# Scores of two query steps at once, and the last queries beside the last keys: a threshold-attention kernel with an ELU feed-forward network on one core

## The chip, the cores and the metric

The kernel runs on one core of one Trainium2 chip. The metric is the device time of one execution in microseconds, taken as the median of several runs. A profiled execution gives, beside it, the span from the first to the last instruction and what each engine did.

## The reference

```python
# q, k, v: (8, 8, 576, 64) fp32; tau: a scalar; w_in (512, 2048), w_out (2048, 512)
scores = scale * np.matmul(q, k.transpose(0, 1, 3, 2))          # scale = 1/8
thresh = np.max(scores, axis=-1, keepdims=True) - tau
scores = np.where(scores >= thresh, scores, -1000000000.0)
attn = np.exp(scores - np.max(scores, axis=-1, keepdims=True))
attn = attn / (np.sum(attn, axis=-1, keepdims=True) + 1e-09)
attn_out = np.matmul(attn, v)
x = attn_out.transpose(0, 2, 1, 3).reshape(4608, 512)           # heads side by side
h = x @ w_in
g = np.where(h > 0.0, h, np.exp(np.minimum(h, 0.0)) - 1.0)      # ELU
out = g @ w_out
```

## The kernel before

**Units of work.** Two heads of one batch entry form a pair; there are 32 pairs, four to a batch entry. A pair has 576 queries: four steps (i = 0 to 3) of 128 queries with both heads, and a fifth (i = 4) that holds the last 64 queries of both heads in one tile of 128 rows (`qd`, a tile with the two 64-row blocks on its diagonal). The last 64 keys of a head are its "last keys".

**One step.** `scores` (L236) writes 2 x 288 columns per head to PSUM; the two heads use the upper and the lower 64 rows of TensorE. Then for each head: VectorE takes the maximum (`max_of`, L276), GpSimd computes the threshold (`bound_of`, L280), ScalarE the bias `nb` (L285) and the exponential into a tile `e` (L287), VectorE masks it into `w` and sums it in one instruction (`mask_of`, L296), then takes the reciprocal (L302, L303), and GpSimd normalizes (L272). A step later `turn_squares` transposes `w` on VectorE in 32 x 32 squares into a tile `x` (L380, L390) and sends it to DRAM in four DMAs (L393); two steps later `fetch` (L401, L403) reads it back as `wTa` (steps 0 and 1) or `wTb` (steps 2 to 4), now with keys on the partitions. `values` multiplies with v in two parts: one matmul for the last keys (L416, `vd` holds the last 64 rows of both heads' v on its diagonal) and eight with 64 output rows (L420). `values_out` copies the result to `xt`.

**FFN.** It works on 512 tokens of a batch entry at a time, with products of half-size blocks (seven products in place of eight). `first_product` (L955) has seven quarters for each of eight blocks, `second_round` (L1110) twice 28; a quarter is two or four matmul records, about 0.86 us of TensorE. A batch entry makes 112 quarters, 28 for each pair. After the products ScalarE and VectorE move them out of three PSUM banks, and exp, minus one and the ELU follow on ScalarE, GpSimd and VectorE (L988, L993, L1002, L1010). Sums of blocks run on GpSimd (L1047) from a queue `extra`; `sums_x` (L846 to L848) on VectorE, once per batch entry.

**Order.** There are stages: the first four pairs alone, some pairs with a plain FFN and the weights' preparation, and from the tenth pair on (step `MIDDLE`) attention of pairs 9 to 31 beside the FFN of batch entries 1 to 6; then FFN alone. In the stage from `MIDDLE` on the order on each engine comes from an agenda: `on_pe(cost, f)` puts work on TensorE and moves a clock by an assumed cost, `at(t, f)` puts the other work in the order of its planned time. The engines then run their lists in order and wait by semaphores. TensorE's order for a pair was

```python
QUARTERS = ((4, 4), (4, 2), (4, 0), (4, 2), (4, 0))   # FFN quarters before and behind the values, per step
on_pe(1.25, lambda: scores(pr, i, hs))                # each step
end = on_pe(3.1 if part else 2.3, lambda: loc.update(out=values(pr, part)))   # behind steps 4 and 2
```

PSUM in this stage holds three banks for the FFN, four for scores (two tiles of two banks) and one for values.

## Time and profile before

| | |
|---|---|
| median of 3 runs | 1367.07 us (1367.02 to 1367.55) |
| profiled execution, first to last instruction | 1366.1 us |
| granted TensorE clock, mean | 0.994 |
| TensorE matmul busy | 1340.4 us (98%) |
| VectorE busy | 1064.7 us (78%) |
| ScalarE busy | 638.5 us (47%) |
| GpSimd busy | 825.2 us (60%) |
| DMA | 259.84 MB, mean 190 GB/s |

A line of a group reads: source line, engine (PE TensorE, PEld its weight loads, DVE VectorE, ACT ScalarE, POOL GpSimd, SP the DMA queue's engine), operation, output and inputs by the program's names, shapes, count, then busy time in us and the mean of one in ns, then idle time before it and what ended that idle time. In the line of a tile `f` is the FFN's PSUM, `sc` the scores', `pv` the values', `rt` that of transposes.

### The profile page before, as it was taken

Reading aid. Unit: us, or ns where it says so; the run is one execution under the profiler, and the core shown is the slowest. Engines: PE = TensorE matmul, PEld = TensorE weight load, DVE = VectorE, ACT = ScalarE, POOL = GpSimd, SP = SyncE. Lnnn points to the kernel's source line nnn. Section 1 sums busy time; section 2 is a strip of 40 time slices with the busy share of each in tenths; the row PEclk is TensorE's granted clock in tenths of the full one; section 3 lists DMA queues with packets and bytes.
Section 4 is the critical chain, followed back from the end, with each engine's and each line's share of the span. In section 5 each row is a group of like instructions: output and inputs, shape, how many; then the busy total and the mean of one; then the engine's idle time right before and its main releaser. Section 6 shows DMA issues by size and latency. Waiting matters only on the chain.

```text
span 1366.1 us, 22394 instructions
## 1 busy us (share of the span) xinstructions
PE 1340.4 (98%) x6796; PEld 1008.9 (74%) x6796; DVE 1064.7 (78%) x2344; ACT 638.5 (47%) x1418; POOL 825.2 (60%) x1322
## 2 busy tenths in 40 slices
PE   8998999999999999999999999999999999999998
PEld 7665746747777777777777777777777777888886
DVE  6879895988888887888798978888898875445433
ACT  5777675226354445545453636363636452412320
POOL 4657673878657574757475747675675646525423
PEclk9999999999999999999999999999999999999999
DMA  5254451688888989798889888897889785412211
GB/s 116 59 108 137 132 151 43 198 247 256 237 251 239 260 229 259 206 267 247 230 234 263 236 238 241 245 269 203 245 225 266 218 258 155 135 59 66 93 59 31
DMA packets 316343, 259.84 MB, mean 190 GB/s; under 512 B 208320, under 2 KB 272320, under 8 KB 316224
## 3 DMA queue, kind: packets, MB, share of 16 engines
q1 hardware_dynamic: 313856, 258.13, 67.6%
q8 instruction: 54, 0.88, 0.3%
q10 hardware_dynamic: 2368, 0.30, 0.2%
q14 instruction: 65, 0.53, 0.1%
HBM read 167.84 MB, written 90.51 MB: 189 GB/s over the span
## 4 chain that ended last, share of the span: by engine, by line
PE 89%; DVE 4%; ACT 2%; POOL 2%; issue 1%; DMA 0%; ACTq 0%; DVEq 0%; POOLq 0%; SPq 0%
PE f L1110 28%; PE f L955 28%; PE sc L236 13%; PE pv L420 9%; PE f L507 3%; PE rt L306 3%; PE pv L416 3%; PE f L467 2%; DVE mx L276 1%; POOL w L272 1%; DVE w L296 1%; ACT e L287 1%; DVE wtop L142 0%; ACT wTa L322 0%; DVE wtop L137 0%
## 5 line engine op out<-in xcount | busy, mean ns | idle before, releaser
L272 POOL TENSOR_SCALAR w<-w,rs 128x576 f32<-128x576 f32 x288 | 248.4, 867 | 120.7 <-DVE rs L303 99.9
L276 DVE TENSOR_REDUCE mx<-sc 128x1 f32<-128x576 f32 x270 | 192.8, 750 | 89.0 <-PE sc L236 88.8
L296 DVE SCALAR_TENSOR_TENSOR w<-sc,th,e 128x576 f32<-128x576 f32 x270 | 212.8, 811 | 26.7 <-ACT e L287 10.0
L287 ACT ACTIVATE e<-sc,nb,keep 128x576 f32<-128x576 f32 x270 | 223.0, 831 | 9.2 <-POOL nb L612 0.7
L285 ACT ACTIVATE nb<-mx,nkeep 128x1 f32<-128x1 f32 x254 | 75.2, 296 | 256.4 <-DVE mx L276 256.4
L380 DVE STREAM_TRANSPOSE x<-w 128x512 f32<-128x512 f32 (+1 forms) x350 | 182.6, 568 | 8.2 <-POOL w L272 8.2
L236 PE MATMUL sc<-kT,qT 64*128 64x288 f32 x1024 | 166.7, 431 | 9.0 <-DVE w L296 6.1
L236 PEld LDWEIGHTS sc<-kT,qT 64*128 64x128 f32 x1024 | 92.8, 187 | 71.4 <-issue 49.4
L280 POOL TENSOR_SCALAR th<-mx,ntau 128x1 f32<-128x1 f32 x270 | 75.7, 281 | 114.0 <-DVE mx L276 113.3
L955 PE MATMUL f<-xt,sw 128*128 128x256 f32 x512 | 128.9, 389 | 0.5 <-DVE g L977 0.5
L955 PE MATMUL f<-xt,w_in_sb 128*128 128x256 f32 x512 | 124.5, 382 | 0.3 <-ACT w L969 0.2
L955 PEld LDWEIGHTS f<-xt,sw 128*128 128x128 f32 x512 | 93.3, 190 | 28.9 <-issue 13.5
L955 PEld LDWEIGHTS f<-xt,w_in_sb 128*128 128x128 f32 x512 | 96.1, 190 | 18.9 <-ACT xs L432 4.6
L1110 PE MATMUL f<-w_out_sb,s 128*128 128x256 f32 x448 | 109.4, 387 | 0.0
L1110 PE MATMUL f<-w_out_sb,g 128*128 128x256 f32 x448 | 107.6, 382 | 0.5 <-DVE g L1010 0.5
L1110 PE MATMUL f<-t,s 128*128 128x256 f32 x448 | 106.6, 380 | 0.3 <-POOL s L1047 0.3
L955 PE MATMUL f<-x,w_in_sb 128*128 128x256 f32 x448 | 105.8, 379 | 0.0
L1110 PEld LDWEIGHTS f<-w_out_sb,s 128*128 128x128 f32 x448 | 82.3, 190 | 23.0 <-issue 11.3
L1110 PEld LDWEIGHTS f<-w_out_sb,g 128*128 128x128 f32 x448 | 83.8, 190 | 16.9 <-issue 4.2
L974 POOL TENSOR_TENSOR u<-u,w 128x256 f32<-128x256 f32 x64 | 48.9, 764 | 76.5 <-ACT u L969 76.5
L1110 PEld LDWEIGHTS f<-t,s 128*128 128x128 f32 x448 | 84.1, 190 | 13.7 <-POOL s L1047 2.7
L955 PEld LDWEIGHTS f<-x,w_in_sb 128*128 128x128 f32 x448 | 85.1, 190 | 11.6
(165 smaller groups left out, 2435.4 us busy)
## 6 DMA issues: line engine op xcount, KB each, us to landing
there<-x SPq DMA_DIRECT2D x500, 144.0 KB, 4.2
wTb<-there SPq DMA_DIRECT2D x75, 576.0 KB, 4.9
wTa<-there SPq DMA_DIRECT2D x50, 576.0 KB, 4.3
sw<-win_sums SPq DMA_DIRECT2D x62, 384.0 KB, 4.6
t<-wout_sums SPq DMA_DIRECT2D x45, 512.0 KB, 5.6
qm<-in_q_dram SPq DMA_DIRECT2D x128, 72.0 KB, 4.2
vm<-in_v_dram SPq DMA_DIRECT2D x64, 128.0 KB, 4.3
wst<-in_moe_w_in_dram SPq DMA_DIRECT2D x16, 512.0 KB, 4.3
```

The lines of the kernel that those rows point to most:

```text
L236: nc.tensor.matmul(scs[h][:, a, :HALF], qs[r], kT[r, k0 : k0 + HALF], start=True, stop=True)
L272: nc.gpsimd.tensor_scalar(wv, wv, st["rs"][:, h : h + 1], 1.0, ALU.mult, ALU.mult)
L276: nc.vector.tensor_reduce(st["mx"][:, h : h + 1], st[h][:, :, :HALF], axis=AX.XY, op=ALU.max)
L280: nc.gpsimd.tensor_scalar(st["th"][:, h : h + 1], st["mx"][:, h : h + 1], 1.0, ntau, ALU.mult, ALU.add)
L285: nc.scalar.mul(st["nb"][:, h : h + 1], st["mx"][:, h : h + 1], nkeep)
L287: nc.scalar.activation(e, st[h][:, :, :HALF], AF.Exp, bias=st["nb"][:, h : h + 1], scale=keep)
L296: nc.vector.scalar_tensor_tensor(wv, sc[:, :, :HALF], st["th"][:, h : h + 1], e, ALU.is_ge, ALU.mult, accum_out=st["sm"][:, h : h + 1])
L380: nc.vector.transpose(x[:, :, c0 : c0 + nc_], src.rearrange("p (c g n) -> p g c n", c=nc_, n=T))
L420: nc.tensor.matmul(pv[h * D : (h + 1) * D, g0 * T : g1 * T], vm[:, h, c], wT[:, g0:g1, h * (NC + 1) + c], start=False, stop=(c == NC - 1), ...
L955: nc.tensor.matmul(loc["banks"][place], left[:, j], right[:, j], start=(begins and j == 0), stop=(j == 1), skip_group_check=True)
L974: nc.gpsimd.tensor_tensor(loc[name], x(), loc[other], op)
L1110: nc.tensor.matmul(place(m), lhs, rhs, start=(begins and v == 0), stop=(v == RU - 1), skip_group_check=True)
```

## The change

It concerns pairs 9 to 31 alone; all before is the same program. Per pair TensorE's order is now: the last queries' scores of this pair together with the last keys' part of the values of the pair two back (`tails_and_values`); that pair's eight and eight main value matmuls; the scores of steps 0 and 1 together (`wide_scores`); 14 quarters; the scores of steps 2 and 3 together; 14 quarters. So a pair's step i = 4 now comes first.

- Scores lie in one PSUM tile of five banks, four times 576 columns side by side. One call has eight matmuls of 64 to 512 columns, upper and lower rows in turns.
- The last queries are no longer a diagonal tile of 128 rows: four 64-by-64 matmuls of 288 columns; the last keys' part of the values is four 64-by-64 matmuls of 256 or 320 columns.
- `on_banks` declares the dependencies on that tile by hand: any two engines that touch the same bank are ordered, readers too. A copy of one element (`seen`, ScalarE) stands between two matmuls that use one bank.
- The exponential is written into the place of `w` and masked there. The two steps of a half use two such tiles, `w` and the former two `e` tiles.
- `turn_squares` takes 640 + 512 columns in place of 512 + 128 + 512 for a main step, with every fourth column going to one 32-row square ("c k g" in place of "c g k"), and one DMA in place of four. For the last queries it is 512 columns and twice 128 in place of twice 512 and twice 64. The read-back comes a pair later.
- ELUs lose the rule that held them back until the masks were through (`late_elus`); the minus one of each second half stays with GpSimd.

The core of the diff:

```diff
+    def wide_scores(pr, half):
+        qT, kT, _ = pairs[pr]
+        for s in range(2):
+            i = 2 * half + s
+            st = open_step(pr, i, turned_by[1 - s])
+            for h in range(2):
+                c = (2 * h + (s ^ h)) * S
+                st["sc", h], st["e", h] = wide[0][:, c : c + S], st["w"][:, h * S : (h + 1) * S]
+        for h, s, c, n in ((0, 0, 0, 512), (1, 1, 0, 384), (0, 0, 512, 64), (1, 1, 384, 192),
+                           (1, 0, 0, 320), (0, 1, 0, 448), (1, 0, 320, 256), (0, 1, 448, 128)):
+            i, r = 2 * half + s, slice(h * D, (h + 1) * D)
+            k0 = c + (0 if h else TAIL)
+            o = open_steps[pr, i]["sc", h][:, c : c + n]
+            on_banks(nc.tensor.matmul(o, qT[r, i * P : (i + 1) * P], kT[r, k0 : k0 + n], start=True, stop=True,
+                                      skip_group_check=True), o)
+            if n == 384:
+                on_banks(nc.scalar.copy(seen, o[:, :1]), o[:, :1])
...
+        for a in range(2):                                   # in tails_and_values
+            for h in range(2):
+                r, x = slice(h * D, (h + 1) * D), a ^ h
+                if pr is not None:
+                    o = sc[D - h * D : P - h * D, x, :HALF]
+                    on_banks(nc.tensor.matmul(o, qT[r, MAIN:], kT[r, TAIL + x * HALF : TAIL + (x + 1) * HALF], start=True,
+                                              stop=True, skip_group_check=True), o)
+                if before is not None:
+                    g0, g1 = span(h, x)
+                    o = pv[r, x, g0 * T : g1 * T]
+                    on_banks(nc.tensor.matmul(o, vd[r, r], parts[x][r, g0:g1, NC], start=True, stop=False,
+                                              skip_group_check=True), o)
...
         def turn_part(c0, src, nc_):
-            nc.vector.transpose(x[:, :, c0 : c0 + nc_], src.rearrange("p (c g n) -> p g c n", c=nc_, n=T))
+            form = "p (c k g) -> p g c k" if pr >= JOINED else "p (c g k) -> p g c k"
+            nc.vector.transpose(x[:, :, c0 : c0 + nc_], src.rearrange(form, c=nc_, k=T))
+        if pr >= JOINED:
+            half = T // 2
+            if i < NC:
+                turn_part(0, w[:, : (NC + 1) * P], NC + 1)
+                turn_part(NC + 1, w[:, (NC + 1) * P :], NC)
+            else:
+                turn_part(1, w[:, :MAIN], NC)
+                tail = w[:, MAIN:S].rearrange("p (k g) -> p g k", g=NT).unsqueeze(2).broadcast_to([P, NT, 2, half])
+                for c in (0, NC + 1):
+                    nc.vector.transpose(x[:, :, c].rearrange("p g (h k) -> p g h k", h=2), tail)
+            n = NCH if i < NC else NC + 2
+            there = turns[pr, i] = dram.tile([P, NT, n * T], FP32, name="there2", bufs=12)
+            nc.sync.dma_start(there, x[:, :, :n].rearrange("p g c n -> p g (c n)"))
+            return
...
+        def tail_step(pr):
+            on_pe(1.2, lambda: loc.update(zip(("main", "outs"), tails_and_values(own, joined))))
+            if own is not None:
+                at(t + 1.25, lambda: wide_max(pr, NC, 0))
+                at(t + 2.0, lambda: wide_bounds(pr, NC))
+                at(t + 2.0, lambda: wide_exp(pr, NC, 0))
+                at(t + 3.3, lambda: wide_mask(pr, NC, 0))
+                finish_of(pr, NC, t + 4.2, t + 10.5)
+            if joined is not None:
+                for part, cost in ((1, 2.2), (0, 1.8)):
+                    end = on_pe(cost, lambda: loc["main"](part))
+                    at(end, loc["outs"][part])
...
+        def wide_step(pr, half):
+            on_pe(2.15, lambda: wide_scores(pr, half))
+            e = t + 2.15
+            for s in range(2):
+                i = 2 * half + s
+                at(e + 1.55 + 1.5 * s, lambda i=i: wide_bounds(pr, i))
+                for h in range(2):
+                    k = 2 * s + (h ^ s)
+                    at(e + 0.75 * k, lambda i=i, h=h: wide_max(pr, i, h))
+                    at(e + (1.6, 3.0, 4.7, 5.6)[k], lambda i=i, h=h: wide_exp(pr, i, h))
+                    at(e + (3.0, 4.3, 6.5, 6.9)[k], lambda i=i, h=h: wide_mask(pr, i, h))
+                finish_of(pr, i, e + (5.1, 7.8)[s], e + (8.4, 10.5)[s])
...
+        HALF_QUARTERS = 14
+        for pr in range(JOINED, NP + 2):
...
+            tail_step(pr)
...
+            ffn_quarters(begin)
+            for half in range(2):
+                if pr < NP:
+                    wide_step(pr, half)
+                ffn_quarters(HALF_QUARTERS - (0 if half else begin))
```

## The prediction

> **What bounds the kernel now.** I read the page first, then busy time by stretch, then TensorE's timeline in one pair, then VectorE's groups by shape and its waits.
>
> ```profile
> span 1366.1 us, 22394 instructions
> ...
> PE 1340.4 (98%) x6796; PEld 1008.9 (74%) x6796; DVE 1064.7 (78%) x2344; ACT 638.5 (47%) x1418; POOL 825.2 (60%) x1322
> ...
> DVE  6879895988888887888798978888898875445433
> ...
> PE 89%; DVE 4%; ACT 2%; POOL 2%; issue 1%; DMA 0%; ACTq 0%; DVEq 0%; POOLq 0%; SPq 0%
> ```
>
> TensorE is busy 98% and 89% of the chain is its own work. VectorE stands at eight or nine tenths just where attention and FFN run together. The timed median is 1367.07 us, 1.0 above this span; I count in the span and add 1.0. About 0.2% (2.7 us) is what a measurement of this kernel can tell from no change.
>
> ```profile
> 814.00:850.00 36.00, 36.00 (x188) 27.26 (x184) 31.14 (x69) 21.97 (x52) 24.80 (x41) 1.00 0.92 261
> 850.00:886.00 36.00, 36.00 (x188) 27.26 (x184) 32.58 (x77) 12.62 (x27) 23.63 (x40) 1.00 0.83 225
> 886.00:922.00 36.00, 36.00 (x188) 27.26 (x184) 31.16 (x69) 21.99 (x52) 24.81 (x41) 1.00 0.94 272
> 922.00:958.00 36.00, 36.00 (x188) 27.26 (x184) 28.94 (x70) 13.34 (x29) 18.65 (x34) 1.00 0.75 205
> ```
>
> Columns: stretch, its length, busy PE, PEld, DVE, ACT, POOL, clock, DMA share, GB/s. Each stretch is one pair. TensorE is busy all of each 36.00 us at full clock: a pair costs what its matmuls cost. VectorE has 31.1, 32.6, 31.2 and 28.9 us of work per pair (mean 31.0), so it has only 5.0 us to spare: that is what this change will be measured against.
>
> ```profile
> 832.64 0.81 PE L416 MATMUL pv<-wTb,vd 128*128 128x384 f32 x2
> 833.38 2.37 PE L420 MATMUL pv<-wTb,vm 128*64 128x320 f32 x16
> 835.68 1.24 PE L236 MATMUL sc<-kT,qT 64*128 64x288 f32 x8
> 836.86 1.13 PE L955 MATMUL f<-xt,w_in_sb 128*128 128x256 f32 x4
> ...
> 842.32 1.13 PE L236 MATMUL sc<-kT,qd 128*128 128x288 f32 x4
> 843.29 1.89 PE L955 MATMUL f<-xt,w_in_sb 128*128 128x256 f32 x8
> ...
> 846.75 0.59 PE L416 MATMUL pv<-wTa,vd 128*128 128x256 f32 x2
> 847.27 1.95 PE L420 MATMUL pv<-wTa,vm 128*64 128x256 f32 x16
> 849.15 1.24 PE L236 MATMUL sc<-kT,qT 64*128 64x288 f32 x8
> ```
>
> From start to next start: scores of a step 1.17 us, last queries 0.97, the two value products 0.74 + 2.30 and 0.52 + 1.88. A matmul has two records (fp32 passes). The 16 records of 320 columns take 2.30, of 256 columns 1.88: in eight pairs that run together, 0.42/8/64 = 0.82 ns a column, and about 0.2 is left for going into the half-array shape. A step's scores agree: 4 pairs x 288 x 0.82 ns = 0.94 of 1.17.
>
> **The change on TensorE, per pair.** The FFN's 28 quarters stay; the chain shows 112 records of them in 24.17 us. So attention now costs 36.00 - 24.17 = 11.83. Its columns are 4 x 0.94 (scores), 0.97 (last queries), 0.52 + 0.74 (last keys' values), 3.78 (values): 9.77. The other 2.06, over six changes of shape, is 0.34 a change (in and out).
> After: the scores have the same columns, 3.78. Last queries and last keys become eight 64-by-64 matmuls in two groups of four, each group two passes of at most 320 columns: 4 x 0.26 = 1.05 if all four run together. Main values 3.78. Entries: two from the FFN at 0.34, two between attention shapes at about 0.2: 1.08. Sum 9.7, a pair 33.9: 2.1 us less. Four quadrants at once are in no row. Bounds: two at a time (as rows have it) 2.10 instead of 1.05, four at a time 1.05; I take 1.05, because the groups differ in both rows and columns, each of which alone overlaps in the rows above. Unequal partners (512 beside 384 columns) cost nothing if each half streams by itself, and 0.21 a half if starts keep step (2560 column times instead of 2304 over both passes); I take nothing, and keep +0.4 a pair.
>
> **VectorE, per pair.** Maxima, masks, sums, ELUs and additions keep number and shape.
>
> ```profile
> L380 DVE STREAM_TRANSPOSE x<-w 128x512 f32<-128x512 f32 x250 | 169.4, 685 | 1.0 <-POOL w L272 1.0
> L380 DVE STREAM_TRANSPOSE x<-w 128x128 f32<-128x128 f32 x100 | 27.4, 274 | 7.2 <-POOL w L272 7.2
> ...
> L390 DVE STREAM_TRANSPOSE x<-w 128x64 f32<-128x64 f32 x50 | 8.2, 201 | 0.0
> ...
> L142 DVE SCALAR_TENSOR_TENSOR wtop<-wst,wtop 128x512 uint32<-128x512 uint32 x32 | 28.9, 904 | 1.0
> L137 DVE TENSOR_SCALAR wtop<-wst 128x512 uint32<-128x512 uint32 x32 | 17.4, 543 | 0.0
> L481 DVE SCALAR_TENSOR_TENSOR g<-g,f 128x512 f32<-128x512 f32 x16 | 10.8, 674 | 7.4 <-POOL g L477 7.4
> ```
>
> A step's transposes go from 512 + 128 + 512 columns (2 x 0.685 + 0.274 = 1.64) to 640 + 512: slope (0.685 - 0.274)/384 = 1.07 ns, so 0.82 + 0.685 = 1.51. Last queries go from 2 x 0.685 + 2 x 0.201 = 1.77 to 0.685 + 2 x 0.274 = 1.23. Together -1.1 us: 29.9 on the mean.
> But these transposes now read every fourth word of w, 16 bytes apart (the "c k g" order), in 4 x 1152 + 640 = 5248 columns per pair. No row reads so. The nearest read every second word: L137, one source, 0.543 for 512 columns, shows no extra; L142, two sources, 0.904 against 0.674 for L481 on plain operands, shows 0.23/512 = 0.45 ns a column. So 0 to 0.45 ns, 0 to 2.4 us a pair; a gain is excluded, since a transpose already moves a column per 1.07 ns and nothing is dropped. I take 2.4: the new step is twice as wide as either row's. VectorE then has 32.3 us of work.
> [...]
>
> **New waits.** The five banks are guarded bank by bank, between readers too: in the built order the fourth maximum of a half waits for ACT's first exponential. That is bounds (0.297) and exponential (0.831), about 1.3 us with signals behind the second maximum, of which the third covers 0.71: 0.6 idle in each half. On the last queries the same chain idles VectorE 1.3, less where an ELU stands between: 1.0. Together 2.1 us of idle a pair that cannot be shifted. Queued behind the wait on VectorE are the masks and the additions that free the FFN's three banks; TensorE waits for those. The one-element copy ("seen") before the eighth score matmul lies on ACT, where only copies whose matmuls are over stand ahead, some 1.3 us before it is needed: nothing, and 0.4 a half if an exponential is ahead. Where the scores follow the values directly, ACT's 0.37 copy of the last part hides beside the first scores' two passes (0.84).
> So VectorE needs 32.3 + 2.1 = 34.4 on the mean: 34.5 in pairs with first products, 33.9 + 2.1 = 36.0 in the heavy pair, 32.3 in the light one. TensorE needs 33.9. The longer of the two, pair by pair, is 34.5, 36.0, 34.5, 33.9: mean 34.7. Since the first additions come just when their bank is due (four maxima, two masks, a transpose, sums and a preparation come first, about 7 us, and the bank is due 6.9 after the scores), I add 0.3: 35.0.
>
> **POOL, ACT, DMA.** POOL loses four bounds (0.28 each) and the copies of the last queries, ACT four (0.30) and gains two copies; both stay under 25 of 35 us. DMA bytes stay; a write is one issue instead of four, and the read-back, one pair later, waits for nothing (SP now waits 136 us there). DMA share goes from 0.86 to about 0.89: off the path while stretches at 0.94 still run at full TensorE.
>
> **The sum.** Stage before: from 307.7 to 1165.9, 858.2 us. After: 21 pairs x 35.0 = 735.0; the first two, with fewer values, 34.0 + 34.5; a pair of FFN and values alone 28.8; the last values and the wait for their sums 6.1. Together 838.4, 19.8 less: 1366.1 - 19.8 + 1.0 = 1347.
>
> **Rivals.**
> (A) The stride costs nothing. Then VectorE has 29.9 + 2.1 = 32.0, TensorE bounds at 33.9, with 0.3 of stalls 34.2: 718 + 30.5 + 33 + 28.8 + 6 = 816.5, so 1325. For it: L137. Against: 16 bytes is a wider step.
> (B) Quadrants two at a time and scores in step: TensorE 33.9 + 1.05 + 0.4 = 35.4, pairs 35.6: 1363. For it: no row has four. Against: both kinds of overlap are there singly.
> (C) Slower: VectorE becomes the bound. One mechanism: the transposes' 16-byte reads. The break-even is 36.0 of need, that is 36.0 - 2.1 - 29.9 = 4.0 us a pair, 0.76 ns a column. At twice today's 1.07 ns they cost 5.6 more: need 37.6, 23 x 37.6 + 34.8 = 899.6, so 1408. For it: VectorE has just 5 us to spare and L142. Against: L137.
> That the change does not do what it says can be excluded: the built order has the joined matmuls from the tenth pair on, and everything before is unchanged.
>
> **How the numbers follow.** Forecast 0.34 (1335 to 1360), A 0.25 (1318 to 1335), B 0.09, C 0.32, most of it between 1368 and 1410 since even a little beyond break-even is slower. Range 1320 to 1402 leaves out some 2 in 10. Faster: forecast, A, and nearly all of B, 0.65; within 0.2%: 0.04, where B and C meet; slower 0.31.
>
> **What would show it.** Pairs 34 to 36 us apart; TensorE's score groups 2.1 us; last queries with last keys 1.2 to 1.4 (2.3: B); transposes of 640 columns at 0.8 (A), 1.1 (forecast) or over 1.3 (C); TensorE's waits naming VectorE's additions. Wrong if TensorE waits longest for ACT or a DMA.

## The result and the profile after

The changed kernel takes 1423.32 us (median; 1418.44 to 1424.79), the kernel before 1367.31 (1367.02 to 1368.02): a ratio of 1.040, 95% interval 1.0385 to 1.042. It is 56 us slower, where the forecast was 20 us faster and the range ended at 1402. The profiled execution spans 1420.6 us at the same granted clock (0.99).

The page of the changed kernel: busy times and the chain that ended last.

```profile
PE 1339.4 (94%) x6980; PEld 1013.7 (71%) x6980; DVE 1137.2 (80%) x2227; ACT 615.9 (43%) x1372; POOL 795.8 (56%) x1188
...
PE 17%; DVE 2%; ACT 1%; issue 1%; POOL 0%; DMA 0%; ACTq 0%; DVEq 0%; POOLq 0%
```

TensorE has no more work than before (1339.4 us against 1340.4), but 81 us of the span in which it does none (26 before). The chain can't be followed back through the stage: it is lost after a fifth of the span. So the waits have to be read directly. Four pairs by stretch (length, then busy PE, PEld, DVE, ACT, POOL, clock, DMA share, GB/s), from one start of the last queries to the next:

```profile
804.03:841.44 37.41, 35.74 (x193) 27.48 (x192) 33.13 (x65) 12.51 (x27) 19.59 (x31) 1.00 0.67 199
841.44:879.42 37.98, 35.32 (x193) 27.08 (x192) 32.86 (x65) 20.60 (x49) 20.68 (x32) 1.00 0.74 224
879.42:916.81 37.39, 35.76 (x193) 27.39 (x192) 33.73 (x67) 11.98 (x25) 23.20 (x36) 1.00 0.74 213
916.81:956.29 39.48, 36.09 (x193) 27.14 (x192) 35.88 (x70) 20.59 (x49) 22.63 (x33) 1.00 0.75 228
```

Pairs that took 36.00 us now take 37.4 to 39.5, at full clock. VectorE went from a mean of 31.0 to 33.9 us a pair, yet it is idle 4.2 of 38.1 us. Neither engine fills the pair. Whom TensorE waits for in the stage, and how long in all, how often and at most:

```profile
PE f L1105 <- ACT u L1119: 18.8, 11, 2.7
PE f L1105 <- DVE g L1127: 8.8, 12, 0.8
PE sc L505 <- ACT xs L581: 5.3, 11, 0.8
```

The first is the FFN's matmul that needs a bank which ACT has to copy out (`u`), once in two pairs; the third is the first wide scores, which need banks that still hold values. VectorE's transposes by shape, first after, then of x1_plain (the same kernel with plain reads):

```profile
L387 DVE STREAM_TRANSPOSE x<-e 128x640 f32<-128x640 f32 x46 | 63.2, 1374 | 0.0
L387 DVE STREAM_TRANSPOSE x<-e 128x512 f32<-128x512 f32 x46 | 49.9, 1084 | 0.0
```

```profile
L386 DVE STREAM_TRANSPOSE x<-e 128x640 f32<-128x640 f32 x46 | 38.7, 842 | 0.9
L386 DVE STREAM_TRANSPOSE x<-e 128x512 f32<-128x512 f32 x46 | 30.8, 670 | 0.0
```

Reading every fourth word costs (1374 - 842)/640 = 0.83 and (1084 - 670)/512 = 0.81 ns a column more. Summed over all transposes of the 21 pairs that the table below covers, the two traces differ by 90.5 us, which is 4.3 us a pair.

TensorE's own part came as forecast. In its timeline (start, duration, line) the last queries (L552) and last keys (L557), and then the values (L565), follow without a gap:

```profile
804.03 0.45 PE L552 MATMUL sc<-kT,qT 64*64 64x288 f32 x1
...
804.05 0.48 PE L557 MATMUL sc<-wTb,vd 64*64 64x320 f32 x1
...
805.16 2.37 PE L565 MATMUL sc<-wTb,vm 128*64 128x320 f32 x16
```

Four quadrants start within 0.02 us, and all sixteen records are through in 1.13. The rest can be told from starts alone. The table gives, for each group on TensorE, the time from its first start to that of the next group, as a mean over the 21 pairs that have all groups; the first row is the least that each group takes anywhere in these kernels.

| us | last queries, last keys | values | first wide scores | 14 quarters | second wide scores | 14 quarters | pair | waits | VectorE busy in four pairs |
|---|---|---|---|---|---|---|---|---|---|
| least | 1.13 | 4.03 | 2.25 | 12.28 | 2.25 | 12.28 | 34.2 | | |
| changed | 1.13 | 4.03 | 3.05 | 13.53 | 2.25 | 14.21 | 38.2 | 4.0 | 33.9 |
| x1_plain | 1.13 | 4.03 | 2.90 | 13.03 | 2.25 | 13.35 | 36.7 | 2.5 | 30.5 |
| x13_narrow | 1.13 | 4.03 | 2.94 | 12.76 | 2.25 | 13.46 | 36.6 | 2.4 | 30.3 |
| x11_plain_narrow | 1.13 | 4.03 | 2.51 | 12.50 | 2.25 | 12.59 | 35.0 | 0.8 | 26.4 |
| x17_plain_swap | 1.13 | 4.03 | 2.57 | 13.03 | 2.25 | 13.54 | 36.5 | 2.3 | 30.3 |

### The profile page after: what moved, and what is told of

The parts are those of the page before. It is cut to its first block, busy times and chain, and to the rows that moved or that the text cites. A ratio compares the mean times of both kernels' runs of the same rounds, so it can differ in the third digit from the quotient of the medians.

```text
span 1420.6 us, 21662 instructions
## 1 busy us (share of the span) xinstructions
PE 1339.4 (94%) x6980; PEld 1013.7 (71%) x6980; DVE 1137.2 (80%) x2227; ACT 615.9 (43%) x1372; POOL 795.8 (56%) x1188
## 5 line engine op out<-in xcount | busy, mean ns | idle before, releaser
L278 POOL TENSOR_SCALAR w<-w,rs 128x576 f32<-128x576 f32 x196 | 176.0, 903 | 150.9 <-DVE rs L309 133.4
L512 DVE TENSOR_REDUCE mx<-sc 128x1 f32<-128x576 f32 x207 | 148.2, 750 | 32.8 <-PE sc L505 18.9
L387 DVE STREAM_TRANSPOSE x<-w 128x512 f32<-128x512 f32 (+2 forms) x143 | 147.4, 1065 | 0.0
L505 PE MATMUL sc<-kT,qT 64*128 64x512 f32 (+6 forms) x736 | 120.3, 425 | 5.3 <-ACT xs L581 5.3
L522 ACT ACTIVATE w<-sc,nb,keep 128x576 f32<-128x576 f32 x115 | 91.4, 829 | 73.8 <-DVE e L526 64.0
L526 DVE SCALAR_TENSOR_TENSOR w<-sc,th,w 128x576 f32<-128x576 f32 x115 | 90.0, 812 | 37.6 <-ACT w L522 30.6
L505 PEld LDWEIGHTS sc<-kT,qT 64*128 64x128 f32 x736 | 83.1, 186 | 46.8 <-issue 16.5
L517 ACT ACTIVATE nb<-mx,nkeep 128x2 f32<-128x2 f32 (+1 forms) x115 | 34.1, 296 | 173.8 <-DVE mx L512 172.7
L387 DVE STREAM_TRANSPOSE x<-e 128x640 f32<-128x640 f32 x92 | 109.2, 1229 | 0.0
L518 POOL TENSOR_SCALAR th<-mx,ntau 128x2 f32<-128x2 f32 (+1 forms) x115 | 32.6, 283 | 121.4 <-DVE mx L512 121.3
```

The costliest lines, as they stand in the source:

```text
L278: nc.gpsimd.tensor_scalar(wv, wv, st["rs"][:, h : h + 1], 1.0, ALU.mult, ALU.mult)
L387: nc.vector.transpose(x[:, :, c0 : c0 + nc_], src.rearrange(form, c=nc_, k=T))
L505: on_banks(nc.tensor.matmul(o, qT[r, i * P : (i + 1) * P], kT[r, k0 : k0 + n], start=True, stop=True, skip_group_check=True), o)
L512: on_banks(nc.vector.tensor_reduce(st["mx"][:, h : h + 1], st["sc", h], axis=AX.XY if i == NC else AX.X, op=ALU.max), st["sc", h])
L517: nc.scalar.mul(st["nb"][:, cs], st["mx"][:, cs], nkeep)
L518: nc.gpsimd.tensor_scalar(st["th"][:, cs], st["mx"][:, cs], 1.0, ntau, ALU.mult, ALU.add)
```

## Experiments

| run | what it is | median, us | ratio to before, 95% |
|---|---|---|---|
| x1_plain | changed, plain reads | 1388.57 | 1.013 to 1.016 |
| x2_strided_before | before, strided reads | 1403.0 | 1.024 to 1.027 |
| x3_late_elu | changed, ELUs later | 1426.55 | 1.0415 to 1.045 |
| x4_plain_late | x1 and x3 | 1388.96 | 1.013 to 1.016 |
| x5_plain_gap | x1, two quarters ahead of the first half | 1399.2 | 1.021 to 1.024 |
| x6_plain_gap_late | x4 and x5 | 1427.99 | 1.042 to 1.046 |
| x7_gap | changed, two quarters ahead | 1438.86 | 1.050 to 1.053 |
| x9_plain_copies | x1, copies ahead of the bound | 1409.7 | 1.028 to 1.032 |
| x8_plain_max4 | x9, fourth maximum first, POOL's sum later | 1419.5 | 1.034 to 1.039 |
| x10_copies | changed, copies ahead of the bound | 1444.19 | 1.052 to 1.058 |
| x11_plain_narrow | x1, masks of 64 columns | 1348.2 | 0.984 to 0.987 |
| x13_narrow | changed, masks of 64 columns | 1385.47 | 1.0105 to 1.014 |
| x12_plain_spread | x1, quarters 7, 14, 7 | 1444.72 | 1.053 to 1.057 |
| x14_plain_turn | x1, one step's transposes later | 1416.94 | 1.033 to 1.037 |
| x15_turn | changed, the same | 1460.0 | 1.065 to 1.070 |
| x16_plain_turn_sums | x14, POOL's sum later | 1408.63 | 1.026 to 1.031 |
| x17_plain_swap | x1, POOL's sum, a normalization and transposes later | 1383.87 | 1.010 to 1.014 |
| x18_plain_best | x17, ELUs later | 1396.09 | 1.019 to 1.024 |

### The strided reads: x1_plain and x2_strided_before

x1_plain is the changed kernel with the old reading order, and so with four write DMAs:

```diff
-            form = "p (c k g) -> p g c k" if pr >= JOINED else "p (c g k) -> p g c k"
-            nc.vector.transpose(x[:, :, c0 : c0 + nc_], src.rearrange(form, c=nc_, k=T))
+            nc.vector.transpose(x[:, :, c0 : c0 + nc_], src.rearrange("p (c g k) -> p g c k", c=nc_, k=T))
...
+            for p in range(NT):
+                nc.sync.dma_start(there[:, :, p].rearrange("c k n -> k c n"), ...)
```

> The changed kernel with transposes that read w in order (c g k, as before) and four DMAs a step again; all else stays. Theory T, the 16-byte reads are the cause: a main step's transposes fall from 2.4 to about 1.5 us, VectorE's work from 33.9 to about 29.8 us a pair, TensorE bounds again at 34 to 34.6 us, and the time is 1325 to 1345 us. Rival R, the new order and its waits are the cause (VectorE idles 4.2 us a pair, ACT's copies come late): pairs stay at 37 us or more, 1385 us or above.

x2_strided_before is the kernel before with only the strided reads and the single write DMA, from the tenth pair on:

```diff
-            nc.vector.transpose(x[:, :, c0 : c0 + nc_], src.rearrange("p (c g n) -> p g c n", c=nc_, n=T))
+            form = "p (c n g) -> p g c n" if pr >= JOINED else "p (c g n) -> p g c n"
+            nc.vector.transpose(x[:, :, c0 : c0 + nc_], src.rearrange(form, c=nc_, n=T))
```

> The kernel before, with the 16-byte reads and the single write DMA alone, from the tenth pair on. T: VectorE gets 3.8 us a pair more, 34.8 of 36.0, so its 5.0 us of room are nearly gone; pairs of 36.0 to 37.5 us, 1367 to 1400 us, likeliest 1378. R: the room absorbs it, 1364 to 1370 us.

Measured 1388.57 and 1403.0. Taking the stride out of the changed kernel gives back 35 us; putting it into the kernel before costs 35 us. Neither theory held alone: the stride explains 35 of the 56 us, and about 21 us belong to the new order, which with plain reads is still slower than before. In both edits the number of write DMAs changes together with the reading order, and no run separates the two; TensorE's waits in the changed kernel name no transfer, and the transposes themselves take longer on VectorE. The same edit was in five more pairs of runs, and always cost much the same: x3 against x4 37.6, x7 against x5 39.7, x10 against x9 34.5, x13 against x11 37.3, x15 against x14 43.1 us.

### Changes of order, one wait at a time: x3 to x10

x3_late_elu moves the ELUs of the second half behind the third maximum, since in the trace the first of them stands ahead of the maxima and ACT's bound, and so of the copy of `u`.

```diff
-                at(now[0] + (2.0 if c and attending[0] else 1.4), lambda: elu(c))
+                at(now[0] + ((2.9 if c else 3.5) if attending[0] else 1.4), lambda: elu(c))
```

> The changed kernel with its ELUs planned 2.1 and 0.9 us later, so that they stand between the third and fourth maximum of a half instead of before the first and third. Nothing else changes; reads stay at 16 bytes. T: VectorE stays the bound, only the idle before the fourth maximum and the ELU's own wait go, 0.5 to 1 us in every other pair: 1410 to 1420 us. R: the bounds, and with them ACT's copies for which TensorE waits 23 us in all, come earlier: 1385 to 1400 us.

x4_plain_late is the same edit on x1_plain.

> The plain reading order of x1_plain, and the ELUs of the second half planned behind the third maximum instead of between the first two and the last two. In x1_plain (1388.57 us) the first bound and exponential of the second half wait 0.6 us for the ELU between the maxima, and TensorE then waits 1.25 us for ACT's copy of u, once in two pairs. Theory U (these waits are TensorE's, and VectorE has room once its reads are plain): the wait for u falls to about 0.5 us, 11 times 0.75 = 8 us less: 1377 to 1384. Rival V (VectorE is still what limits, and a job moved comes back elsewhere, as in x3_late_elu): 1387 to 1393.

Neither gained anything: 1426.55 beside 1423.32, and 1388.96 beside 1388.57. The groups on TensorE show why. In x4 the quarters behind the second wide scores fall from 14.15 to 13.15 us in the pairs with first products, as theory U had it, and rise from 12.47 to 13.73 in the others, where the late ELUs hold up POOL's sums for the second round (TensorE's wait for POOL `s`: 8.7 us in all). In x3 it is 15.33 to 14.32 and 12.99 to 14.06.

x5_plain_gap puts two FFN quarters between the values and the first half, so that ACT has emptied the values' banks in time; x7_gap does so with strided reads, x6_plain_gap_late together with the late ELUs.

```diff
-            begin = 4 if pr == JOINED else 0
+            begin = 4 if pr == JOINED else 2
```

> x1_plain with two FFN quarters (1.8 us) between the main values and the first wide half, and 12 instead of 14 behind it. In x1_plain the first wide half takes 3.62 instead of 2.25 us in every second pair: its third pair of matmuls waits for banks that ACT still has to empty of values, behind the exponential of the last queries. Theory U (the place where the values' banks come free costs 1.37 us in every second pair): 11 times 1.37 = 15 us less, 1372 to 1377. Rival V (VectorE limits, the wait turns up at a later addition): 1385 to 1392.

> x4_plain_late and x5_plain_gap together: plain reads, two quarters between values and the first wide half, late ELUs. Theory U: both savings add, 15 + 8 = 23 us less than x1_plain: 1363 to 1369, beside 1367 of the kernel before. Rival V: 1385 to 1393.

> The changed kernel, its strided reads kept, with two FFN quarters between the main values and the first wide half. Its trace has 1.55 us of waiting there in every second pair and 0.54 in every fourth. Theory S (with the strided reads VectorE's chain of waits sets the pair, so a wait of TensorE taken away at one place returns at the next addition): 1417 to 1424, as 1423. Rival (the place itself costs): 11 x 1.55 + 5 x 0.54 = 20 us less: 1400 to 1407.

In x5 the first wide scores take 2.25 us in every pair, as they should, and the kernel is 11 us slower. TensorE's waits say where it came back:

```profile
PE f L1107 <- ACT u L1121: 25.1, 22, 1.8
```

The wait for `u` now comes 22 times instead of 12 (25.1 us instead of 16.1): the first half no longer begins at a product's first quarter, so its exponentials stand ahead of a copy that TensorE needs, in every pair. The theories by which the wait comes back elsewhere were nearer, but too low as well: all three times lie above every range (x6 by 35 us).

x9_plain_copies plans the first bound and exponential of a half 0.35 us later, behind the FFN's copy of `u` or `s` on ACT; x10_copies is the same with strided reads. x8_plain_max4 adds two more orders to x9.

```diff
-                at(e + 1.55 + 1.5 * s, lambda i=i: wide_bounds(pr, i))
+                at(e + 1.9 + 1.15 * s, lambda i=i: wide_bounds(pr, i))
...
-                    at(e + (1.6, 3.0, 4.7, 5.6)[k], lambda i=i, h=h: wide_exp(pr, i, h))
+                    at(e + (1.95, 3.0, 4.7, 5.6)[k], lambda i=i, h=h: wide_exp(pr, i, h))   # x8: 2.3 first
...
-            extras(e + 0.3, e + 1.2, e + 4.2, e + 10.4, e + 12.0)
+            extras(e + 0.3, e + 1.2, e + 4.2, e + 11.2, e + 12.0)                           # x8 alone
```

> x1_plain (1388.57 us), and on ACT the FFN's copy of u (or of s in the second product) ahead of the first bound and exponential of a half instead of behind them. In x1_plain ACT reaches the copy 2.6 us after its matmuls ended, since the bound waits for VectorE's maxima, and TensorE waits 1.25 us for it (1.63 from start to start), once in two pairs. Theory U (ACT's order makes TensorE wait there): the wait goes, and the second half's FFN falls from 14.12 to some 12.6 us in every second pair: 11 times 1.5 = 16 us less, 1370 to 1377. Rival V (VectorE's chain sets the pace, the exponentials now come later and the wait is given back at additions): 1385 to 1395.

> x9_plain_copies, and two more orders: the first exponential of a half behind the fourth maximum, so that the maximum waits for no shared bank (0.56 to 0.7 us of VectorE's idle in each half of x1_plain), and one of POOL's sums for the FFN behind the difference t that VectorE's addition ahead of the last queries' maximum waits for (in x1_plain it stands in front and costs 0.7 us in every second pair, at whose end the first wide scores wait 1.37 us). Theory U: x9's saving and 11 times 0.7 = 8 us more: 1362 to 1370. Rival V: 1385 to 1395.

> The changed kernel with its strided reads (1423.3 us) and the order on ACT of x9_plain_copies. Its second halves take 14.91 to 16.5 us of FFN in every second pair and 13.1 in the others, instead of 12.34. Theory S (the strided reads leave VectorE behind, so that TensorE then waits for additions instead): 1416 to 1424. Rival U (ACT's order alone): 11 times 1.8 = 20 us less, 1400 to 1406.

In x9 TensorE's wait for `u` is gone from the list, and the kernel is 21 us slower. VectorE's wait of a maximum for the exponential on a shared bank went from 10.8 to 34.8 us, and TensorE waits for additions instead (`g` 12.6, `ot` 10.3 us). The wait of the maxima, in x1_plain and then in x9:

```profile
DVE mx L514 <- ACT e L524: 10.8, 18, 0.7
```

```profile
DVE mx L514 <- ACT e L524: 34.8, 23, 2.8
```

x8 and x10 are slower still. So ACT's order is no free choice: what goes ahead there for TensorE holds back VectorE through the bank guards.

### VectorE's load: x11_plain_narrow and x13_narrow

Both keep every instruction, its order and its waits, and shorten the masks alone (with a maximum in place of the product, so that the short sums stay positive). A mask then covers 64 of 576 columns: the rest of the probabilities is neither masked nor summed, so part of the softmax is left out.

```diff
+        few = (slice(None), slice(None), slice(0, 32)) if i == NC else (slice(None), slice(0, 64))
+        e, sc = st["e", h][few], st["sc", h][few]
-        on_banks(nc.vector.scalar_tensor_tensor(st["e", h], st["sc", h], st["th"][:, h : h + 1], st["e", h], ALU.is_ge,
-                                                ALU.mult, accum_out=st["sm"][:, h : h + 1]), st["sc", h])
+        on_banks(nc.vector.scalar_tensor_tensor(e, sc, st["th"][:, h : h + 1], e, ALU.is_ge,
+                                                ALU.max, accum_out=st["sm"][:, h : h + 1]), st["sc", h])
```

> x1_plain (1388.57 us) with masks of 64 columns instead of 576: every instruction, its order and its waits stay, but VectorE's ten masks of a pair take some 0.15 instead of 0.81 us, 6.6 us of VectorE's time less a pair (the probabilities are left unmasked, so that part of the softmax is not computed). In x1_plain a pair takes 36.7 us, of which 34.34 are TensorE's own. Theory D (the waits come from VectorE's busy time between the scores and the copies and additions that TensorE needs): pairs fall to 34.4 to 34.8, 1388.6 - 21 x 2.1 = 1344; 1338 to 1352. Rival L (they come from the links of the chain, maxima to bound to exponential to mask, and from the order on ACT, whatever VectorE is busy with): 1375 to 1390.

> The changed kernel with its strided reads (1423.3 us) and masks of 64 columns instead of 576 (part of the softmax is not computed): VectorE's work falls from 33.9 to some 27.3 us a pair, against 34.34 of TensorE's own. Theory D (VectorE's busy time): 1423 - 21 x 3.6 = 1347; 1340 to 1365. Rival L (links and order of the new chain): 1400 to 1420.

x11 takes 1348.2 us, theory D; x13 takes 1385.47, between the two. A mask fell from 0.81 to 0.27 us, which is 4.9 us for a pair's masks (nine, not ten as I had written), and VectorE's busy time by 4.0 (x11) and 3.6 us (x13). TensorE's longest wait in the stage, of x11 and then of x13:

```profile
PE f L1109 <- ACT u L1123: 3.7, 12, 1.7
```

```profile
PE f L1107 <- ACT u L1121: 20.3, 12, 2.7
```

With plain reads the wait for `u` nearly goes; with strided ones it stays, though VectorE is then idle 6.3 of 36.6 us. So neither reading was whole. As I read it, VectorE's time is what makes TensorE wait, but as queue ahead of certain jobs, not as a sum that has to fit into the pair. The table in the section above shows a regularity: x1_plain and x13_narrow got to the same VectorE time by quite different edits (30.5 and 30.3 us) and have the same pair (36.7 and 36.6); from 26.4 over 30.4 to 33.9 us of VectorE, pairs go 35.0, 36.6, 38.2. That is (38.2 - 35.0)/(33.9 - 26.4) = 0.43 us of pair for each us of VectorE, long before VectorE is full.

This slope holds for this one order alone. The other arrangements with plain reads and full masks (x12 aside) all have 30.0 to 30.6 us of VectorE's work a pair as a mean over the 21 pairs, and their pairs take from 36.5 us (x17) to 38.4 (x6). And in the old order as much work costs no wait at all. Four pairs of the kernel before, and then of x2_strided_before (columns as in the windows above):

```profile
590.33:734.29 143.96, 143.96 (x738) 109.05 (x737) 123.72 (x284) 69.92 (x158) 91.92 (x154) 1.00 0.86 241
```

```profile
601.61:751.64 150.03, 147.55 (x737) 110.11 (x736) 141.56 (x280) 70.22 (x158) 92.49 (x155) 1.00 0.77 232
```

With 30.9 us of VectorE's work a pair TensorE is busy without a break; with 35.4 the pairs take 37.5 us. The new order waits already at 26.4.

x12_plain_spread moved the first half away from the values.

```diff
-            begin = 4 if pr == JOINED else 0
+            begin = 4 if pr == JOINED else 7
...
-                ffn_quarters(HALF_QUARTERS - (0 if half else begin))
+                ffn_quarters(7 if half else 14)                        # pairs behind the first joined one
```

> x1_plain with the FFN quarters of a pair placed 7, 14 and 7 (between values and first half, between the halves, behind the second half) instead of 0, 14 and 14. Both halves still begin at a product's first quarter. Theory P (the first half is too near to the last queries and to the values' banks): the 1.37 us at the first wide scores go in every second pair and nothing comes back, 1370 to 1378. Rival V (the order of the FFN's copies and additions against the halves sets the waits, and any shift costs, as in x5_plain_gap): 1392 to 1415.

It takes 1444.72 us and decides nothing. With seven quarters behind the second half, the next pair's last queries come before that half's second step is transposed, and write into the same tile (so part of the probabilities is lost); TensorE then waits 16.4 us for the next pair's `kT` and 32.0 for VectorE's work on `w`, which no theory had.

### Where the chain begins: x14 to x18

This is the wait for `u` in x1_plain, in order of time (start, duration, then engine and line; in brackets idle time before and what ended it):

```profile
840.43 1.18 POOL L278 TENSOR_SCALAR w<-w,rs 128x576 f32<-128x576 f32 x1
...
842.26 0.73 POOL L1126 TENSOR_TENSOR t<-g,u 128x256 f32<-128x256 f32 x1
...
843.03 0.42 DVE L1129 TENSOR_TENSOR g<-f,t 128x256 f32<-128x256 f32 x1
...
843.55 0.63 ACT L1137 ACTIVATE ge<-g 128x512 f32<-128x512 f32 x1 [1.00 <-DVE g L1129]
...
844.88 0.69 DVE L1157 SCALAR_TENSOR_TENSOR g<-ge,g 128x512 f32<-128x512 f32 x1 [1.09 <-ACT ge L1149]
...
845.49 1.42 DVE L514 TENSOR_REDUCE mx<-sc 128x1 f32<-128x576 f32 x2
...
846.94 0.29 ACT L519 ACTIVATE nb<-mx,nkeep 128x2 f32<-128x2 f32 x1 [1.31 <-DVE mx L514]
...
848.00 0.36 ACT L1121 COPY u<-f 128x256 f32<-128x256 f32 x1
...
848.41 1.13 PE L1107 MATMUL f<-xt,w_in_sb 128*128 128x256 f32 x4 [1.25 <-ACT u L1121]
```

The copy's matmuls ended at about 845.4. It stands on ACT behind a bound that needs two maxima; the maxima stand on VectorE behind an ELU; the ELU needs ACT's exponential, that needs VectorE's addition, that needs POOL's difference `t`, and `t` stands on POOL behind a normalization. In between, from 841.65 to 843.03, VectorE transposes (2.31 instead of 1.44 us with strided reads).

x14_plain_turn takes these transposes out of VectorE's queue at that place; x15_turn does so with strided reads; x16_plain_turn_sums also moves one of POOL's sums behind `t` ahead of the last queries.

```diff
-                finish_of(pr, i, e + (5.1, 7.8)[s], e + (8.4, 10.5)[s])
+                finish_of(pr, i, e + (5.1, 7.8)[s], e + (8.4, 10.5 if half else 16.9)[s])
...
-            extras(e + 0.3, e + 1.2, e + 4.2, e + 10.4, e + 12.0)
+            extras(e + 0.3, e + 1.2, e + 4.2, e + 11.2, e + 12.0)      # x16 alone
```

> x1_plain (1388.57 us) with the transposes of a first half's second step (1.44 us, and 0.65 of idle for POOL's product ahead of them) planned behind the fourth maximum of the second half instead of ahead of the FFN's two additions just before that half. In the traces these stand in one chain: transposes, additions, ACT's exponential and subtraction for the ELU, ELU, maxima, bound, exponential, copy of u, TensorE. Theory Q (what stands ahead of this chain in VectorE's queue sets TensorE's wait, not VectorE's sum over the pair): the chain begins 2.1 us earlier, the wait of 1.25 us in every second pair goes: 11 times 1.4 to 1.8 = 15 to 20 us less, 1368 to 1375. Rival V (any shift costs as much elsewhere): 1385 to 1405.

> The changed kernel with its strided reads (1423.3 us) and the same move: transposes of the first half's second step (2.31 us) behind the fourth maximum of the second half. Theory Q: the second half's FFN falls from 14.9 to 16.5 us to some 12.8 in every second pair, 11 times 2.3 = 25 us less: 1392 to 1405. Rival V: 1418 to 1440.

> x14_plain_turn, and one of POOL's sums for the FFN behind the difference t that VectorE's additions ahead of the last queries' maximum wait for. Theory Q: these additions come 0.7 us earlier in every second pair, and with them the copies that free the values' banks, for which the first wide scores wait 1.37 us: 11 times 0.7 = 8 us less than x14_plain_turn, 1360 to 1368. Rival V: no gain beside x14_plain_turn, or a loss.

(In the first joined pair, which has ten quarters there, these three transpose one step after it is overwritten; the other pairs are computed in full.) x14 is 28 us slower than x1 and x15 37 slower than the changed kernel: theory Q as I had it fell. With the transposes gone VectorE just waits for `t` (27.1 us in all instead of 7.8), the wait for `u` falls only from 16.1 to 14.2 us, and 1.44 us of work have moved to where they delay the additions. x16 is 8.3 us faster than x14, the difference that was expected, if not the time: the first wide scores fall from 3.61 to 2.93 us in every second pair. So the other wait, for the values' banks, does begin on POOL. In x1_plain, where POOL's sum still stands ahead, ACT comes late to the copies that free those banks, because the last queries' exponential is late:

```profile
790.25 0.83 ACT L524 ACTIVATE w<-sc,nb,keep 128x576 f32<-128x576 f32 x1
790.99 0.36 ACT L577 COPY xt<-sc 128x256 f32<-128x256 f32 x1
791.24 0.43 ACT L583 COPY xs<-sc 64x64 f32<-64x64 f32 x2
```

The matmuls of the part that is copied first had ended by 788.7; the second of the eight matmuls of the wide scores starts at 791.81, when `xs` is out.

x17_plain_swap takes all this together on x1: POOL's sum behind `t`; where first products stand between the halves, also the normalization behind `t` and its transposes behind the third maximum. x18_plain_best adds later ELUs for all but the last product of a round.

```diff
-                at(t_sum + 0.25 + 0.75 * h, lambda h=h: normalize(pr, i, [h]))
+                at(t_sum + 0.25 + (0.75 + later) * h, lambda h=h: normalize(pr, i, [h]))
...
+            coming = running[0] if quarters or not queue else queue[0][0]
+            first = half or pr == JOINED or coming is not first_product
...
-                finish_of(pr, i, e + (5.1, 7.8)[s], e + (8.4, 10.5)[s])
+                finish_of(pr, i, e + (5.1, 7.8)[s], e + (8.4, 10.5 if first else 15.95)[s], 2.3 if s and not first else 0.0)
...
-                at(now[0] + (2.0 if c and attending[0] else 1.4), lambda: elu(c))                        # x18
+                late = attending[0] and v < RU - 1
+                at(now[0] + ((2.9 if c else 3.5) if late else 2.0 if c and attending[0] else 1.4), lambda: elu(c))
```

> x1_plain (1388.57 us) with three moves, each ahead of one TensorE wait. On POOL the sum for the FFN goes behind the difference t ahead of the last queries (as in x16_plain_turn_sums, where the first wide scores fell from 3.62 to 2.92 us). Where first products stand between the halves, the first half's last normalization (1.18 us) goes behind t on POOL too, and the transposes that read it behind the third maximum of the second half on VectorE. In x14_plain_turn moving only the transposes left the wait for u at 14.2 us in all, since VectorE's additions then waited for t on POOL. Theory Q (the chain begins on POOL: normalization, t, additions, exponential and subtraction, ELU, maxima, bound, exponential, copy of u): the additions come 1.2 us earlier and the wait for u nearly goes, 11 times 1.2 to 1.6 = 13 to 18 us, and 11 times 0.7 = 8 at the first wide scores: 1362 to 1370. Rival V (any shift comes back as other waits): 1385 to 1410.

> x17_plain_swap, and the ELUs of all but the last product of a round planned behind the third maximum, so that the first bound of the second half waits for two maxima alone. Theory Q: what is left of the wait for u goes, and with the last product's ELUs left where they are, the sums for the second round are not late as they were in x4_plain_late: 1358 to 1367. Rival V: no gain beside x17_plain_swap, or a loss of up to 10 us.

x17 takes 1383.87 us, 4.7 less than x1_plain and the shortest of those that compute everything in the new order, but 1.2% above the kernel before. The gain is near the noise: x17's runs lie from 1383.53 to 1385.77, x1_plain's from 1384.53 to 1389.29. TensorE's waits in its stage:

```profile
PE f L1107 <- DVE g L1129: 9.1, 23, 1.2
PE f L1107 <- ACT u L1121: 7.9, 12, 1.8
```

The first wide scores gave their 0.7 us (3.62 to 2.92 in every second pair, 11 times 0.7 = 7.7 us). The wait for `u` fell to half (from 16.1 us), but the additions `g`, which had 3.1 us, now have 9.1, and the quarters behind the second half went from 14.15 to 14.52 us in these pairs. x18 removes the rest of the wait for `u` and loses 12 us to POOL's sums and later copies. Both theories had a part: the waits at the first wide scores do begin on POOL, and most of what is taken out of the chain comes back elsewhere.

## Why the prediction was wrong

**What held.** TensorE's attention takes 1.13 + 4.03 + 2.25 + 2.25 = 9.66 us a pair, forecast 9.7: four quadrants do run at once (1.13; forecast 1.05 and an entry), unequal partners cost at most 0.15 us a half (2.25; forecast 2.1), and rival B's 2.3 us are excluded. Going back into the FFN costs 0.19 a half on top, 12.28 instead of 12.09, which the 9.7 was meant to include, so that TensorE's own pair is 34.2, not 33.9. TensorE's gain shows once VectorE is relieved: x11_plain_narrow, which leaves most of the masking out, is 20 us faster than the kernel before. That it lands beside the forecast's 1347 is luck: its VectorE works 26.4 us a pair, not 32.3.

**The strided reads, a term mis-sized.** I took 0.45 ns a column, 2.4 us a pair, from L142, a two-source row with a step of two words; measured are 0.81 to 0.83 ns and 4.3 us, above the 0.76 ns from which rival C decided. The row did not show what I read from it. I had its mean, 0.904 us; in the kernel before its shortest, median and longest are:

```profile
L142 DVE SCALAR_TENSOR_TENSOR wtop<-wst,wtop x32: 680/694/1809, 28.0 to 208.2; 128x512 uint32<-128x512 uint32 x32
```

Of the 32, 24 take 0.68 to 0.70 us, and the other eight, 1.04 to 1.81 us, all ran beside a GpSimd instruction (L148 or L272). Against 0.676 for the plain row L481 a step of two words cost next to nothing. So no row of the old trace gave a price for the step of four, and that my 2.4 was not farther off is luck. Rival C named the strided reads, and x1 and x2 price them at 35 us of the 56 in both orders; but VectorE did not become the bound, as C has it, since it idles 4.3 us a pair.

**The step that failed: "the longer of the two, pair by pair".** The sum set VectorE's work plus 2.1 us of idle against TensorE's 33.9 and took the larger. With the measured 4.3 for the stride that step gives 29.9 + 4.3 + 2.1 = 36.3 us a pair, some 1375; measured are 38.2. A pair with 33.9 us of VectorE's work has 4.3 of VectorE's idle time, and 4.0 of TensorE's beyond its own 34.2: neither of the two is the bound. Forecast for the stalls behind an exact bound was 0.3. In this order the pair costs 0.43 us more for each us of VectorE already at 26 us of work. The traces fit the reading that what counts is what stands in the queues ahead of an addition, a maximum or a copy that TensorE waits for soon; no run isolates it. Of the 1423 - 1347 = 76 us, 21 x (38.2 - 35.0) = 67 lie in the 21 pairs; the rest lies in the first two joined pairs, 39.6 + 37.8 us instead of 34.0 + 34.5.

**"The ACT copy hides beside the first scores": wrong.** I counted its 0.37 us, not what stands ahead of it: the last queries' exponential, which waits for a maximum, which stands behind additions, which wait for POOL. The first wide scores lost 0.8 us a pair by it in the changed kernel, 0.65 in x1_plain.

**The bank guards.** That the fourth maximum waits for the first exponential was foreseen (0.6 a half; 13.2 us over 28 waits, 0.47 each). Not foreseen was that the guards tie ACT's order to VectorE's, so that x9's order, better for TensorE's copies, cost 21 us. A version without guards between readers wasn't tried, so what it would give isn't shown.

**"Wrong if TensorE waits longest for ACT or a DMA."** It does: 18.8 us for ACT's `u`. DMA share fell to 0.67 to 0.75 instead of rising to 0.89 (x1_plain, with four writes a step, has 0.79 to 0.86), and none of TensorE's waits names a transfer.

What stays open: I can name the chain behind the two waits that I followed, but found no arrangement in which the new order pays. Of ten other arrangements with plain reads and the same shapes, one is faster than x1_plain, by 4.7 us; whether another has more isn't shown.

## What to carry to other kernels

When work is put into larger batches on an engine that takes its jobs in order (in x1_plain ACT sat idle for 1.31 us ahead of a bound, with the copy of `u` ready behind it), don't compare its busy sum with the bound: follow, for each batch, the queue ahead of the jobs that release the bounding engine's buffers, across all engines. Here, in the new order, each us on VectorE cost 0.43 us of time while VectorE was still idle for a quarter; in the old order 30.9 us of its work cost none. Price a strided read by a row with the same stride and the same instruction, or by running that one edit in the old kernel, which here settled 35 of 56 us. And look at the shortest and the median of a row before using its mean: a few long instructions (here eight of 32, 1.04 to 1.81 us beside a GpSimd instruction, against 0.68 to 0.70) can look like a stride's price.

## What the runs showed of the hardware

- A 32 x 32 transpose on VectorE that reads every fourth fp32 word took 1.37 us for 640 columns (changed kernel) against 0.84 (x1_plain), and 1.08 against 0.67 for 512; in the old order the mean of all 250 of 512 columns, 20 of them ahead of the tenth pair and plain, was 1.067 (x2_strided_before) against 0.685 in the kernel before. Reading every second word with a two-source instruction cost next to nothing (L142 in the kernel before, uint32: 0.694 us at the median, against 0.676 of the plain fp32 row L481).
- Eight fp32 matmuls of 64 x 64 with 256 to 320 columns, two records each, took 1.13 us with the four quadrants at work at the same time (changed kernel, from 804.03 to 805.16).
- In x1_plain an ELU took 0.67 us where it started ahead of a GpSimd instruction, and 1.17 where it started 0.10 us behind one (the difference `u`). A GpSimd normalization took 0.74 us on the mean of the 88 of the tile `e`, 1.11 where it started 0.18 us behind an ELU, and 1.18 beside the second ELU, from 840.43 on:

```profile
837.88 0.67 DVE L1157 SCALAR_TENSOR_TENSOR g<-km,g 128x512 f32<-128x512 f32 x1
...
838.06 1.11 POOL L278 TENSOR_SCALAR w<-w,rs 128x576 f32<-128x576 f32 x1 [1.82 <-DVE rs L309]
...
839.73 0.72 POOL L1126 TENSOR_TENSOR u<-u,w 128x256 f32<-128x256 f32 x1
...
839.83 1.17 DVE L1157 SCALAR_TENSOR_TENSOR g<-ge,g 128x512 f32<-128x512 f32 x1
```

The first ELU above takes 0.67 us, and the normalization that starts 0.18 us behind it 1.11. The second ELU starts 0.10 us behind the difference `u`, which ends 0.62 us after the ELU's start, and takes 1.17. No run isolates why these are longer. What both engines lose there, 0.50 us (1.17 - 0.67) on the second ELU and 0.37 and 0.44 (1.11 and 1.18 - 0.74) on the two normalizations, is part of the queue that the prediction did not count.
